# Attention gated by a token mixer on one core: one turn of four PSUM banks for scores and block products, block pairs spread over the steps in new orders, and a first chunk that is normalised in two halves

## The chip, the core and the metric

The kernel runs on one core of a Trainium2 chip. PE is the matrix engine, DVE the vector engine, ACT the scalar engine, POOL GpSimd, SP the engine whose queue issues most DMAs. The metric is the time of one execution on the device in microseconds, as the median of several runs. Durations inside the kernel come from one profiled execution.

## What is computed

S = 2048 tokens, D = 512 channels, 32 heads of 16, F = 1792. With xn = layernorm(x):

```python
s = attention(xn, wqkv) @ wo            # 32 heads, full softmax over 2048 keys, scale 16 ** -0.5
h = layernorm(xn)
u = gelu(einsum("sd,sf->df", h, w1) + b1)     # the MLP acts along the tokens
y = (einsum("df,fs->ds", u, w2) + b2).T
out = x + s * silu(y)
```

All is float32. Matrix products take each operand as an upper part (rounded for the matrix engine, F32R) and a lower part (the rest), and sum three products: upper by upper, upper by lower, lower by upper.

## The kernel before

**Stages.** (1) For each of four chunks of 512 tokens: normalise x on DVE (`Norm`), turn it with PE transposes (L268, `turned`), split it into `xt` (upper by ACT, lower by DVE), multiply by wq and wk (L303, eight groups of 12 products), split the results (`sg`) and store them; then the V products (`three`, L86 to L88). The weights' upper halves are copied by ACT, their lower halves subtracted by POOL (L79). (2) A lead of 11 steps in which row maxima of the first scores are found. (3) The steady part. (4) The drain: the remaining scores, values and products with wo. (5) The tail: the last pair of heads.

**A step of the steady part** covers two score tiles t (128 keys by 1024 queries, two heads a = 0, 1). It holds 8 score products (L777, called s: heads in the two row halves of the array, 50 rows each), each read by one exponential on ACT (L782); 8 products for row maxima of a later pair of heads (L394, called m), each read by one reduction on DVE (L398); twice the products with the values (L793, `values`), which use four column strips of the array; and up to six pairs of block matmuls (L944, called D, two row halves of 64). Two instructions in opposite row halves run side by side, so a step is written as two strings of letters, one for each half, which are read off in pairs; two indices in `ORDERS`, `ENDS` or `BEGINS` say where the values stand. `take` draws the block pairs from a generator, `count` says how many.

**Blocks.** `mixer` makes 14 blocks of the first MLP product (48 pairs each, `gelu`) and 16 of the second (42 pairs, `silu`). `rest` makes `PARTS` = 13 blocks of the attention's output product from the first three groups of heads (9 pairs, `part`, stored to `y_d`), and in the drain one product for each of 16 token blocks, 12 matmuls where no part was made, 3 where one was (`finish`, L753). A block adds up in one PSUM bank and is then emptied by ACT or DVE. At a block's end a step takes no further pairs.

**Banks.** PSUM has eight banks here: pools `ps_sc` (3, scores), `ps_mx` (3, maxima), `ps_av` (1, values), `ps_dn` (1, blocks). Stage 1 takes all eight in turn (`bank`).

**What sets the order.** The code is issued as written, each engine works off its queue in order, and semaphores order the engines. The step tables are written by hand. Lists `later` and `soon` hold work that `run_later` issues at the two places of a step.

Of the kernel before, what the change touches and what calls it, by code (L numbers as in the profile page):

```python
# [21 lines left out]
def tile_attention_token_mixer(ctx, tc, x, wqkv, wo, w1, b1, w2, b2, out):  # L22
# [131 lines left out]
    with (  # L154
        tc.tile_pool(name="pw", bufs=1) as pw,
        tc.tile_pool(name="px", bufs=5) as px,
        tc.tile_pool(name="pt", bufs=6) as pt,
# [23 lines left out]
        for part in range(3):  # L181
            for kd in range(ND):
                nm = ("raw", "wh", "wl")[(part * ND + kd) % 3]
# [4 lines left out]
        def w_upper(part):  # L188
            for kd in range(ND):
                nc.scalar.copy(wh[part][:, kd, :], raw_w[part, kd])  # L190

        def w_lower(part):
            for kd in range(ND):
                sub(nc.gpsimd, wl[part][:, kd, :], raw_w[part, kd], wh[part][:, kd, :])

        class Norm:


            def __init__(self, src, dst, then=None):
                self.src, self.dst, self.then = src, dst, then  # L200
# [7 lines left out]
            def rsqrt(self):  # L208
                ve = pst.tile([P, 4], F32, name="ve")
                r = self.r = pst.tile([P, 4], F32, name="r")  # L210
                t = pst.tile([P, 4], F32, name="t")
                nc.vector.tensor_scalar(ve, self.mv[:, :, 1], 1e-5, None, op0=OP.add)
                nc.scalar.sqrt(t, ve)
                nc.vector.reciprocal(r, t)
# [14 lines left out]
            def pieces(self):  # L229
                for b in range(4):  # L230
                    yield lambda b=b: self.stats(b)
                yield self.rsqrt
                for b in range(4):
                    yield lambda b=b: self.apply(b)

        def first(c):
# [4 lines left out]
            return Norm(lambda b: xr[4 * c + b], dst)  # L241
# [11 lines left out]
        def bank():  # L253

            i = turn_of[0] = (turn_of[0] + 1) % 8
            pl, nm = ((ps_sc, "sc"), (ps_mx, "mx"), (ps_dn, "dn"), (ps_av, "av"))[i % 2 if i < 6 else i - 4]
            return pl.tile([P, 512], F32, name=nm)

        for f in first(0).pieces():
            f()  # L260
        w_upper(0)
        xts_ = [[] for _ in range(NC)]

        def turned(c, db):
# [4 lines left out]
            t = pt.tile([P, 2, 512], F32R, name="xt")  # L269
            nc.scalar.copy(t[:, 0, :], ps)  # L270
            sub(nc.vector, t[:, 1, :], ps, t[:, 0, :])
            xts_[c].append(t)

        for c in range(NC):
            cs = slice(c * 512, (c + 1) * 512)
            for db in range(len(xts_[c]), ND):
                turned(c, db)
            if c == 0:

                nc.gpsimd.tensor_copy(pst.tile([P, 1], F32, name="hold"), xn[3][:, :1])  # L280
                w_upper(1)
                w_lower(0)
                w_lower(1)
# [5 lines left out]
            if c == 0:  # L289
                w_upper(2)  # L290
                w_lower(2)
# [35 lines left out]
            for f in todo[len(order) * per :]:  # L327
                f()
# [11 lines left out]
            pv = [bank()[:, :D] for _ in range(4)]  # L340
            if c + 1 < NC:
                for kd in range(ND):
                    for b in range(4):
                        v_product(b, kd)
                    if 0 < kd < ND - 1:
                        turned(c + 1, kd + 1)
            for b, ps in enumerate(pv):
# [5 lines left out]
                else:  # L353
                    v48 = pt.tile([P, 2, 512], F32R, name="xt").bitcast(F32).rearrange("p a b -> p (a b)")
                    v48 = v48[:, : NP * 48].rearrange("p (a b c) -> p a b c", b=3, c=DH)
                nc.gpsimd.memset(v48[:, :, 1, :], 1.0)
                nc.scalar.copy(v48[:, :, 0:3:2, :], ps.rearrange("p (a b c) -> p a b c", b=2, c=DH))
                nc.sync.dma_start(v_d[4 * c + b], v48.rearrange("p a b c -> p (a b c)"))
# [76 lines left out]
    def mixer():  # L435
        n = 0
        ub = []
        for i in range(NF + NB):
            nk = NB if i < NF else NF
            before = i < min(N_BEFORE, NF)  # L440
            if before and i % 2:
                ps = ps_av.tile([P, 512], F32, name="av")[:, :D]
            else:
                ps = ps_dn.tile([P, 512], F32, name="dn")[:, :D]
            for kb in range(nk):
# [5 lines left out]
                if i == NF and kb == NF - 1:  # L451
# [4 lines left out]
                    yield None  # L456
# [696 lines left out]
```

## Time and profile before

| | |
|---|---|
| median of 3 runs | 1667.26 us (1667.24 to 1667.9) |
| profiled execution | 1667.68 us, its span 1665.9 us |
| granted clock of PE, mean | 0.999 |
| PE busy | 1644.1 us, 11700 matmul records |
| DVE, ACT, POOL busy | 1426.0, 1194.2, 569.9 us |
| DMA | 155.30 MB, mean 93 GB/s |
| first chunk's PE work begins | 9.80 us |
| steady part | 216.40 to 1587.00 us |
| last value products begin | 1646.07 us |

The profile gives each group of instructions by line, engine, operation and names (out<-in), its busy time, the mean length of one in ns, and the idle time before it with what ended it. In the rows of stretches stand: the stretch and its length, then for each engine (PE, PE's weight loads PEld, DVE, ACT, POOL) busy time and number of instructions, the granted clock, the mean DMA share and GB/s. Rows in order of time give start, length, engine, line, names, shapes, count, and idle time with its releaser. A product with values shows as two matmul records, every other product as one.

### The profile page before, as it was taken

Reading aid. Unit: us, or ns where it says so; the run is one execution under the profiler, and the core shown is the slowest. Engines: PE = TensorE matmul, PEld = TensorE weight load, DVE = VectorE, ACT = ScalarE, POOL = GpSimd, SP = SyncE. Lnnn points to the kernel's source line nnn. Section 1 sums busy time; section 2 is a strip of 40 time slices with the busy share of each in tenths; the row PEclk is TensorE's granted clock in tenths of the full one; section 3 lists DMA queues with packets and bytes.
Section 4 is the critical chain, followed back from the end, with each engine's and each line's share of the span. In section 5 each row is a group of like instructions: output and inputs, shape, how many; then the busy total and the mean of one; then the engine's idle time right before and its main releaser. Section 6 shows DMA issues by size and latency. Waiting matters only on the chain.

```text
span 1665.9 us, 30703 instructions
## 1 busy us (share of the span) xinstructions
PE 1644.1 (99%) x11700; PEld 871.3 (52%) x11700; DVE 1426.0 (86%) x2482; ACT 1194.2 (72%) x2295; POOL 569.9 (34%) x671
## 2 busy tenths in 40 slices
PE   7999999999999999999999999999999999999997
PEld 6887645545545445554545454554545454444443
DVE  6555988888999899999999999999999999899945
ACT  3332277777777777777877777777777778888875
POOL 4223763433344332331322332222222322642420
PEclk9999999999999999999999999999999999999999
DMA  6468521415133141916151513224051515362346
GB/s 228 165 241 206 115 80 46 72 42 84 49 61 72 34 69 46 247 56 106 36 84 36 96 41 54 57 46 74 21 83 44 103 37 86 119 131 94 107 140 224
DMA packets 152175, 155.30 MB, mean 93 GB/s; under 512 B 51596, under 2 KB 109964, under 8 KB 148956
## 3 DMA queue, kind: packets, MB, share of 16 engines
q1 hardware_dynamic: 147612, 152.59, 38.1%
q8 instruction: 92, 1.51, 0.4%
q0 software_dynamic: 4416, 0.75, 0.3%
q14 instruction: 55, 0.45, 0.1%
HBM read 101.86 MB, written 50.32 MB: 91 GB/s over the span
## 4 chain that ended last, share of the span: by engine, by line
PE 96%; DVE 2%; DMA 1%; ACT 1%; issue 0%; POOL 0%; SPq 0%; DVEq 0%; POOLq 0%
PE av L793 30%; PE dn L944 23%; PE mx L394 17%; PE sc L777 13%; PE dn L903 3%; PE mx L303 2%; PE sc L303 2%; DVE mxp L398 1%; PE av L903 1%; PE dn L303 1%; PE av L303 1%; ACT prob L782 1%; PE mx L777 0%; PE sc L86 0%; PE sc L88 0%; PE sc L87 0%
## 5 line engine op out<-in xcount | busy, mean ns | idle before, releaser
L398 DVE TENSOR_REDUCE mxp<-mx 128x1 f32<-128x512 f32 x2004 | 1244.6, 684 | 134.9 <-PE mx L394 93.8
L782 ACT ACTIVATE prob<-sc 128x512 f32<-128x512 f32 x2004 | 1044.8, 605 | 296.2 <-PE sc L777 182.2
L777 PE MATMUL sc<-big 50*128 50x512 f32 x2004 | 755.6, 417 | 0.5
L394 PE MATMUL mx<-big 48*128 48x512 f32 x2004 | 738.6, 418 | 0.9
L793 PE MATMUL av<-prob,vp 128*32 128x512 f32 x4096 | 545.6, 605 | 0.0
L944 PE MATMUL dn<-hu,wh 64*128 64x512 f32 x1556 | 535.0, 404 | 0.0
L394 PEld LDWEIGHTS mx<-big 48*128 48x128 f32 x2004 | 358.6, 185 | 270.6 <-DVE mxp L398 248.7
L777 PEld LDWEIGHTS sc<-big 50*128 50x128 f32 x2004 | 358.6, 185 | 104.1 <-ACT prob L782 83.5
L944 PE MATMUL dn<-hu,wl 64*128 64x512 f32 x778 | 316.3, 407 | 0.0
L944 PEld LDWEIGHTS dn<-hu,wh 64*128 64x128 f32 x1556 | 284.4, 184 | 44.9 <-issue 23.8
L944 PEld LDWEIGHTS dn<-hu,wl 64*128 64x128 f32 x778 | 143.6, 185 | 108.1 <-issue 78.8
L793 PEld LDWEIGHTS av<-prob,vp 128*32 128x32 f32 x4096 | 80.9, 108 | 177.0 <-issue 166.1
L79 POOL TENSOR_TENSOR wl<-raw,wh 128x512 fp32r<-128x512 f32 x124 | 150.7, 1218 | 38.6 <-ACT wh L150 30.0
L148 POOL CAST wh<-raw 128x512 fp32r<-128x512 f32 (+1 forms) x107 | 62.1, 581 | 260.1 <-PE dn L944 177.7
L421 POOL CAST m<-f 16x128 fp32r<-16x128 f32 x32 | 9.0, 281 | 280.4 <-DVE f L410 280.4
L480 POOL TENSOR_TENSOR sq<-u 128x512 f32<-128x512 f32 x14 | 14.6, 1041 | 177.8 <-ACT u L479 177.8
L83 POOL DMA_DIRECT2D big<-m x128 | 67.7, 535 | 0.0
L944 PE MATMUL dn<-wh,hu 64*128 64x512 f32 x156 | 55.4, 408 | 0.0
L516 POOL TENSOR_SCALAR t<-t 128x512 f32<-128x512 f32 x16 | 23.8, 1490 | 79.9 <-ACT t L513 79.9
L79 POOL TENSOR_TENSOR hu<-hx,hu 128x512 fp32r<-128x512 f32 x16 | 20.3, 1291 | 53.5 <-ACT hu L246 53.5
L782 ACT ACTIVATE prob<-mx 128x512 f32<-128x512 f32 x44 | 28.1, 639 | 13.7 <-PE sc L777 13.6
L303 PE MATMUL mx<-xt,big 128*128 128x512 f32 x144 | 35.9, 399 | 0.0
(205 smaller groups left out, 1117.0 us busy)
## 6 DMA issues: line engine op xcount, KB each, us to landing
raw<-in_B_w_dram SPq DMA_DIRECT2D x104, 256.0 KB
big<-k_d SPq DMA_DIRECT2D x96, 128.0 KB
big<-q_d SPq DMA_DIRECT2D x96, 128.0 KB
q_d<-sg SPq DMA_DIRECT2D x16, 512.0 KB
k_d<-sg SPq DMA_DIRECT2D x16, 512.0 KB
num_d<-ev SPq DMA_DIRECT2D x30, 256.0 KB
u_d<-uo SPq DMA_DIRECT2D x14, 512.0 KB
hu<-u_d SPq DMA_DIRECT2D x14, 512.0 KB
```

What stands on the lines that cost most here:

```text
L79: eng.tensor_tensor(out=o, in0=a, in1=b.bitcast(F32), op=OP.subtract)
L83: queue.dma_start(dst.bitcast(F32), src.bitcast(F32))
L148: nc.gpsimd.tensor_copy(whs[n][:, :m, :], raws[n][:, :m, :])
L303: nc.tensor.matmul(ps, w[part][:, kd, m], xt[kd][:, z, :], start=w is wh and z == 0 and kd == 0, stop=w is wl and kd == ND - 1,)
L394: nc.tensor.matmul(ps, q[o : o + 48, r * P : (r + 1) * P], k[o : o + 48, c * 512 : (c + 1) * 512], start=True, stop=True,)
L398: nc.vector.tensor_reduce(mxp[u // 16][:, a, r % 8, c : c + 1], ps, axis=AX.X, op=OP.max)
L516: nc.gpsimd.tensor_scalar(t, t, 1.0, None, op0=OP.add)
L777: nc.tensor.matmul(ps, ks[p][o : o + 50, kb * P : (kb + 1) * P], qs[p][o : o + 50, at : at + 512], start=True, stop=True,)
L782: nc.scalar.activation(e, ps, AF.Exp, scale=scale)
L793: nc.tensor.matmul(av[32 * j : 32 * j + 32, :], vps[p][:, kb, 16 * a : 16 * a + 32], prob.pop((t, a, c)), start=kb == 0, stop=kb == NB - 1,)
L903: nc.tensor.matmul(ps, w(slice(0, P)), m(slice(0, P)), start=first, stop=last)
L944: made.append(lambda r=r, start=first and a == lead, stop=last and a != lead: nc.tensor.matmul(ps, w(r), m(r), start=start, stop=stop,))
```

## The change

1. **One turn of four banks.** `ps_dn` goes; `ps_sc` has four banks, each a pool of one, taken in turn. A block holds the bank that stands first in the turn (`hold`) and gives it back at the turn's end when the instruction that empties it is issued.
2. **Blocks over steps.** `count` spreads what is left of a block evenly over steps; only three blocks take six pairs in every step. The tables for a block's beginning and end go; `ORDERS` has new strings. The Tanh of `silu` is issued one `run_later` later. The last load of the second product's operand stands two rows earlier, two idle draws behind it go. `PARTS` is 14.
3. **The first chunk.** The V weights are loaded first. 36 transposes of the identity into an unused bank open PE's work (`busy`), some more stand between the first products. Token blocks 0 and 1 are normalised, turned (a block at a time, into all four rows of `xt`), split and multiplied by the V weights before blocks 2 and 3 have been turned. Eleven of twelve lower halves of the weights move from POOL to DVE. `xt` tiles are pairs (3 of double size for 6).

```diff
-    ps_sc = pool("ps_sc", 3, space=PSUM)
-    ps_mx = pool("ps_mx", 3, space=PSUM)
-    ps_av = pool("ps_av", 1, space=PSUM)
-    ps_dn = pool("ps_dn", 1, space=PSUM)
+    class Banks:
+        def __init__(self, name, n):
+            self.free = [pool(f"{name}{i}", 1, space=PSUM) for i in range(n)]
+        def tile(self, shape, dtype, name):
+            self.free.append(self.free.pop(0))
+            return self.free[-1].tile(shape, dtype, name=name, tag="ps")
+        def hold(self, name):
+            p = self.free.pop(0)
+            return p.tile([P, 512], F32, name=name, tag="ps"), lambda: self.free.append(p)
+    ps_sc = Banks("ps_sc", 4)
+    ps_mx = Banks("ps_mx", 3)
+    ps_av = Banks("ps_av", 1)
...
+        def block_turn(b):
+            ps = bank()
+            for db in range(ND):
+                nc.tensor.transpose(ps[:, db * P : (db + 1) * P], xn[b][:, db * P : (db + 1) * P], ident)
+            return ps
...
+        busy(36)
+        one, two = first(0, range(2)), first(0, range(2, 4))
+        for f in one.pieces():
+            f()
...
+        ps0 = block_turn(0)
+        ps1 = block_turn(1)
+        busy(8)
+        two.stats(2)
+        two.stats(3)
+        w_upper(2, [0])
+        block_upper(0, ps0)
+        two.root()
+        w_upper(2, [1])
+        block_lower(0, ps0)
+        w_upper(2, [2])
+        block_upper(1, ps1)
+        two.refine()
+        w_upper(2, [3])
+        for b in (2, 3):
+            two.apply(b)
+        block_lower(1, ps1)
+        w_lower(2, range(ND), nc.vector)
+        for kd in range(ND):
+            v_part(0, 0, wh, [kd])
+            busy((4, 4, 2, 0)[kd])
+        ps2 = block_turn(2)
+        v_part(1, 0, wh, range(ND))
+        ps3 = block_turn(3)
+        v_part(0, 1, wh, range(ND))
+        v_part(1, 1, wh, range(ND))
...
+        w_lower(0, range(1, ND), nc.vector)
+        w_upper(1)
+        w_lower(1, range(ND), nc.vector)
...
             if c == 0:
-                w_upper(2)
-                w_lower(2)
+                for b in range(2):
+                    v_out(b, pv[b], v48s[b], True)
                 nc.sync.dma_start(b1t, b1.rearrange("(b p) -> p b", p=P))
                 nc.sync.dma_start(b2t, b2.rearrange("(b p) -> p b", p=P))
                 nc.vector.tensor_scalar(b2h, b2t, 0.5, None, op0=OP.mult)
...
-                ps = ps_dn.tile([P, 512], F32, name="dn")[:, :D]
+                ps, back = ps_sc.hold("dn")
...
-                if i == NF and kb == NF - 1:
+                if i == NF and kb == NF - 3:
                     while NF - 1 not in stored:
                         yield None
                     ub.append(hu.tile([P, 2, D], F32R, name="hu"))
                     move(ub[NF - 1], u_d[NF - 1])
-                    yield None
-                    yield None
...
-        nc.scalar.activation(t, y, AF.Tanh)
+        later.append(lambda: nc.scalar.activation(t, y, AF.Tanh))
...
-    PARTS = NB // 2 + 5
+    PARTS = NB // 2 + 6
...
-    FULL = range(4, 8)
+    FULL = range(4, 7)
...
-        6: ("DDDDDDsmmsmsms", "msmssmmsDDDDDD", 4, 8),
+        6: ("DDDDDDsmsmsmsm", "smsmmsmsDDDDDD", 4, 8),
...
-        return 4 if late or left in (7, 8) else 5 if left == 9 else max(0, min(6, left))
+        if left == 9:
+            return 4
+        return min(6, -(-left // -(-3 * left // 16))) if left > 0 and i not in FULL else max(0, min(6, left))
```

What this moves in the engines' queues, at three places. First PE at the end of a 42-pair block, before: from the old block's last row to the first of the new one (dn is the block's bank, av the values, mx and sc the maxima and scores; rows of both halves in the order of issue).

```order
L944 MATMUL dn<-hu,wl 128x512
L793 MATMUL av<-prob,vp 32x512 x4
L394 MATMUL mx<-big 128x512
L777 MATMUL sc<-big 128x512 x2
L394 MATMUL mx<-big 128x512
L777 MATMUL sc<-big 128x512
L394 MATMUL mx<-big 128x512
L793 MATMUL av<-prob,vp 32x512 x4
L394 MATMUL mx<-big 128x512
L777 MATMUL sc<-big 128x512
L944 MATMUL dn<-hu,wh 128x512
```

The same place after, with buffer numbers, since the two blocks' rows would read alike (L1050 is the block matmul, L892 a score, L510 a maximum):

```order
L1050 MATMUL dn_14940<-hu_10155,wh_15028 128x512
L510 MATMUL mx_15595<-big_1398,big_1397 128x512
L1050 MATMUL dn_14940<-hu_10155,wl_15029 128x512
L1050 MATMUL dn_15602<-hu_8915,wh_15263 128x512
L892 MATMUL sc_15610<-big_1397,big_1398 128x512
L1050 MATMUL dn_15602<-hu_8915,wh_15263 128x512
L510 MATMUL mx_15615<-big_1398,big_1397 128x512
L1050 MATMUL dn_15602<-hu_8915,wl_15264 128x512
L892 MATMUL sc_15619<-big_1397,big_1398 128x512
```

The new block's first matmul (dn_15602) now follows the old one's last (dn_14940) at once, where two groups of products with values and eight others stood between them.

Second, PE at the start, before:

```order
L268 MATMUL mx<-ident,xn 128x128 x4
L268 MATMUL sc<-ident,xn 128x128 x4
L268 MATMUL mx<-ident,xn 128x128 x4
L268 MATMUL sc<-ident,xn 128x128 x4
L303 MATMUL mx<-xt,big 128x512 x12
L303 MATMUL dn<-xt,big 128x512 x12
```

And after (L331 are transposes of the identity, L304 those of a token block, L344 V products, L412 the products with wq and wk):

```order
L331 MATMUL mx<-ident 128x128 x36
L304 MATMUL sc<-ident,xn 128x128 x4
L304 MATMUL mx<-ident,xn 128x128 x4
L331 MATMUL mx<-ident 128x128 x8
L344 MATMUL sc<-wvh,xt 128x512
L331 MATMUL mx<-ident 128x128 x4
L344 MATMUL sc<-wvh,xt 128x512
```

Twenty-four V products and the turning of blocks 2 and 3 now stand ahead of the first group of twelve.

Third, DVE around the scaling of b2 (`b2h`), which waits for a small DMA. Before:

```order
L222 TENSOR_SCALAR xn<-xr,mv,r 128x512 x4
L79 TENSOR_TENSOR xt<-mx,xt 128x512
L79 TENSOR_TENSOR xt<-sc,xt 128x512
L79 TENSOR_TENSOR xt<-mx,xt 128x512
L79 TENSOR_TENSOR xt<-sc,xt 128x512
L294 TENSOR_SCALAR b2h<-b2t 128x16
L79 TENSOR_TENSOR sg<-mx,sg 128x512
```

After:

```order
L94 TENSOR_TENSOR big<-wl,big 128x512
L94 TENSOR_TENSOR big<-raw,big 128x512
L94 TENSOR_TENSOR big<-wh,big 128x512
L94 TENSOR_TENSOR big<-wl,big 128x512
L403 TENSOR_SCALAR b2h<-b2t 128x16
L94 TENSOR_TENSOR sg<-sc,sg 128x512
```

Lower halves of the weights (big, wvl) now stand in DVE's queue ahead of `b2h`, and the load of b2 stands behind two stores of v in SP's queue.

More of the change, by code (lines that the diff above doesn't have):

```diff
@@ L229, in pieces, with first @@
             def pieces(self):
-                for b in range(4):
+                for b in self.some:
                     yield lambda b=b: self.stats(b)
                 yield self.rsqrt
-                for b in range(4):
+                for b in self.some:
                     yield lambda b=b: self.apply(b)
-        def first(c):
+        def first(c, some=range(4)):
             def dst(b):
@@ new lines, in v_out, with busy @@
+        def v_out(n, ps, v48, ones_in=False):
+            if not ones_in:
+                nc.gpsimd.memset(v48[:, :, 1, :], 1.0)
+            nc.scalar.copy(v48[:, :, 0:3:2, :], ps.rearrange("p (a b c) -> p a b c", b=2, c=DH))
+            nc.sync.dma_start(v_d[n], v48.rearrange("p a b c -> p (a b c)"))
+        v48s = [pst.tile([P, NP, 3, DH], F32, name="v48", bufs=2) for _ in range(2)]
+        for v48 in v48s:
+            nc.gpsimd.memset(v48[:, :, 1, :], 1.0)
+        idle = bank()
+        def busy(n):
+            for _ in range(n):
+                nc.tensor.transpose(idle[:, :P], ident, ident)
@@ new lines, in tile_attention_token_mixer, with v_part @@
+        busy(36)
+        one, two = first(0, range(2)), first(0, range(2, 4))
+        for f in one.pieces():
+            f()
+        pair = [pt.tile([P, 2, 2, 512], F32R, name="xt") for _ in range(2)]
+        xts_[0] = [pair[db // 2][:, db % 2] for db in range(ND)]
+        done_db[0] = ND
+        pv = [bank()[:, :D] for _ in range(2)]
+        def v_part(b, z, w, kds):
+            for kd in kds:
+                nc.tensor.matmul(
+                    pv[b], xts_[0][kd][:, z, b * P : (b + 1) * P], w[2][:, kd, :],
+                    start=w is wh and z == 0 and kd == 0, stop=w is wl and kd == ND - 1,
+                )
@@ L1000, in tile_attention_token_mixer @@
             steady[0] = True
-            late = ended[0]
-            one, two, then = halves(lead, count(late))
+            one, two, then = halves(lead, count())
             made = [dict(D=part, m=heads[a][0], s=heads[a][1]) for part, a in ((one, lead), (two, 1 - lead))]
-            first, second, *places = order(len(one), t, late, bool(then))
+            first, second, *places = order(len(one))
             if one:
@@ L1018, in tile_attention_token_mixer @@
                         of[kind].pop(0)()
-                if "D" in kinds and not two:
-                    for f in then:
-                        f()
-                    then = []
             for f in then:
```

152 lines of the change are left out of this document (84 added, 68 removed).

## The prediction, made before the changed kernel was run

> **What bounds the kernel now.** I read the page first, then the busy time stage by stage, then the order of time on PE, ACT and DVE at a block's end, at the start and near the end. The page, with columns as in its legend:
>
> ```profile
> span 1665.9 us, 30703 instructions
> ...
> PE 1644.1 (99%) x11700; PEld 871.3 (52%) x11700; DVE 1426.0 (86%) x2482; ACT 1194.2 (72%) x2295; POOL 569.9 (34%) x671
> ...
> PE 96%; DVE 2%; DMA 1%; ACT 1%; issue 0%; POOL 0%; SPq 0%; DVEq 0%; POOLq 0%
> ...
> L398 DVE TENSOR_REDUCE mxp<-mx 128x1 f32<-128x512 f32 x2004 | 1244.6, 684 | 134.9 <-PE mx L394 93.8
> L782 ACT ACTIVATE prob<-sc 128x512 f32<-128x512 f32 x2004 | 1044.8, 605 | 296.2 <-PE sc L777 182.2
> ```
>
> PE carries the chain. But its busy time is modelled and overlapping, so 99% does not say that no time is lost: what counts is the pitch of its matmuls. The steady part, from the first attention products at 216.40 to 1587.00, cut at block ends; first all engines, then the block matmuls (L944) alone:
>
> ```profile
> 216.40:269.52 53.12, 53.00 (x399) 26.41 (x398) 47.05 (x80) 40.64 (x80) 19.64 (x23) 1.00 0.17 51
> 269.52:407.43 137.91, 137.91 (x1058) 70.00 (x1056) 122.15 (x208) 104.54 (x203) 53.55 (x63) 1.00 0.31 61
> 407.43:709.99 302.56, 302.39 (x2301) 151.24 (x2299) 272.90 (x467) 231.94 (x448) 109.80 (x132) 1.00 0.38 84
> 709.99:770.89 60.90, 60.58 (x439) 28.26 (x439) 54.88 (x93) 47.52 (x93) 18.96 (x23) 1.00 0.27 60
> 770.89:1436.23 665.34, 665.08 (x5068) 332.43 (x5067) 607.44 (x1034) 521.61 (x1004) 200.33 (x252) 1.00 0.34 66
> 1436.23:1587.00 150.77, 149.96 (x1105) 70.28 (x1104) 138.25 (x236) 125.96 (x244) 65.98 (x65) 1.00 0.40 107
> ```
>
> ```profile
> 216.40:269.52 53.12, 28.98 (x104) 17.91 (x104) 1.00 0.17 51
> 269.52:407.43 137.91, 79.52 (x289) 49.73 (x288) 1.00 0.31 61
> 407.43:709.99 302.56, 157.82 (x578) 100.78 (x577) 1.00 0.38 84
> 709.99:770.89 60.90, 25.09 (x88) 15.14 (x88) 1.00 0.27 60
> 770.89:1436.23 665.34, 343.12 (x1256) 219.48 (x1256) 1.00 0.34 66
> 1436.23:1587.00 150.77, 65.57 (x238) 42.82 (x238) 1.00 0.40 107
> ```
>
> Each step holds 16 halves of scores and maxima and 16 products with values, so (all minus L944)/32 is the number of steps: 9, 24, 54, 11, 119, 27, in all 244. Half of the L944 count is block pairs, some 1276. Now one 42-pair block's length with its end, on PE, DVE and ACT (start, length):
>
> ```profile
> 1268.53 1.06 PE L793 MATMUL av<-prob,vp 128*32 128x512 f32 x8
> ...
> 1296.95 1.07 PE L793 MATMUL av<-prob,vp 128*32 128x512 f32 x8
> ...
> 1302.21 1.06 PE L793 MATMUL av<-prob,vp 128*32 128x512 f32 x8
> ...
> 1304.76 0.39 PE L944 MATMUL dn<-hu,wl 64*128 64x512 f32 x1
> ...
> 1308.33 0.40 PE L944 MATMUL dn<-hu,wh 64*128 64x512 f32 x1
> ...
> 1313.23 1.06 PE L793 MATMUL av<-prob,vp 128*32 128x512 f32 x8
> ```
>
> ```profile
> 1298.52 4.94 DVE L398 TENSOR_REDUCE mxp<-mx 128x1 f32<-128x512 f32 x8 [0.51 <-PE mx L394]
> ```
>
> ```profile
> 1305.70 0.71 ACT L512 ACTIVATE ev<-dn,b2h 128x512 f32<-128x512 f32 x1
> 1306.44 0.63 ACT L513 ACTIVATE t<-ev 128x512 f32<-128x512 f32 x1
> ```
>
> From 1268.53 to 1296.95 lie five six-pair steps: 5.68 us each. A warm 512-wide matmul takes 0.227 (rows of the start, below). My yardstick for a step without loss is 5.68, less 0.227 for each pair short of six. A 42-pair block, eight steps long (1268.53 to 1313.23), took 44.70; by the yardstick 45.44 - 6 x 0.227 = 44.08. So 0.62 is lost, all at the block's end: the old block's last matmul starts at 1304.76, the new one's first only at 1308.33, because both use the one dn bank, which ACT empties at 1305.70; the Tanh behind it keeps ACT from the exponentials.
>
> The same sum by stage (steps x 5.68 - missing pairs x 0.227, against the length): lost 1.8, 1.6, 4.7, 3.6, 8.7 and 6.9, together 27.3 us. That is all that banks and orders can win here. The fourth stage, the change from first to second weights, is where steps hold 1 or 2 pairs.
>
> **The change, part by part.**
>
> Banks. The next block takes the score bank that has been free longest, the old one goes last in the turn. It no longer waits for ACT's emptying. What is late next: scores. While a block is open they have three banks, as before; at a block's end their turn begins with the bank of the last step's seventh of eight scores. By the new order its score stands some 0.9 us ahead of its next use; from the matmul's start to the end of the exponential I take about 0.45 (a matmul's 0.39, 1304.76, and a hand-over) + 0.6 (L782's mean), so 0.1 to 0.2 us is lost. The third score, on the emptied bank, stands behind the next product with values, over 2 us later, and ACT's 0.71 fits. I take 0.2 for each of 40 block ends (1 + 3 + 7 + 16 + 13): 8.0. Bounds: 0, and 0.62 as now.
>
> Tanh one turn later: the same ACT work, under the products with values; nothing of its own.
>
> Spread and orders. The number of steps is the same. The 42 pairs go 6, 6, 5, 5, 5, 5, 5, 5 instead of 6 x 6, 4, 2. A five-pair step by the yardstick is 5.45, above DVE's eight reductions in a row (4.94, the row at 1298.52). DVE is busy 607.44 of 665.34 and stays below PE. In the new orders for five and for six pairs the maxima stand five in a row at two-slot distance, then three behind the product with values, as in the old six-pair order whose steps are the yardstick; so I take no loss for them. Bounds: 0 and 0.1 a step, what a 5.45 step would lose if reductions and the 0.6 of transposes beside them came in a bad place. One block (the eighth) goes from eight steps to nine, the change of weights from about 1.5 pairs a step to full steps, so the steps come out even; its 3.6 goes too.
>
> Parts (last stage): 14 blocks of 9 pairs instead of 13, alternating 4 and 5. Beside the block ends I leave 2.8 here, for ACT's copies of quotients, which stay where they are. Steady part: 27.3 - 8.0 - 2.8 = 16.5 won. The 4 pairs more that now fit into it cost 4 x 0.227 = 0.9. The added part block's copy (ACT, about 0.6), two POOL operations, a load pair and a store on SP's queue lie under PE; the DMA share there is 0.40.
>
> The start. Rows of POOL, DVE and PE:
>
> ```profile
> 1.01 0.29 POOL masks.py:199 TENSOR_SCALAR_AFFINE_SELECT ident<-ident 128x128 f32<-128x128 f32 x1
> ```
>
> ```profile
> 4.94 0.18 DVE L206 BATCH_NORM_AGGREGATE mv<-st 128x2 f32<-128x6 f32 x1
> ...
> 7.66 0.17 DVE L212 TENSOR_SCALAR ve<-mv 128x4 f32<-128x4 f32 x1
> ...
> 9.12 1.91 DVE L222 TENSOR_SCALAR xn<-xr,mv,r 128x512 f32<-128x512 f32 x4
> ...
> 22.22 0.29 DVE L294 TENSOR_SCALAR b2h<-b2t 128x16 f32<-128x16 f32 x1 [6.75 <-DMA b2t<-in_B_b_dram]
> ...
> 31.41 0.54 DVE L222 TENSOR_SCALAR xn<-xr,mv,r 128x512 f32<-128x512 f32 x1
> ```
>
> ```profile
> 9.80 1.75 PE L268 MATMUL mx<-ident,xn 128*128 128x128 f32 x4 [9.80 <-DVE xn L222]
> ...
> 12.21 1.06 PE L268 MATMUL mx<-ident,xn 128*128 128x128 f32 x4
> 13.06 1.06 PE L268 MATMUL sc<-ident,xn 128*128 128x128 f32 x4
> ...
> 17.81 2.89 PE L303 MATMUL dn<-xt,big 128*128 128x512 f32 x12
> ...
> 36.87 0.60 PE L268 MATMUL mx<-ident,xn 128*128 128x128 f32 x4
> ```
>
> Twelve products take 2.89 at 17.81, the last of them some 0.39, so 0.227 each. But the first transposes go at 0.213 (four in 0.85), twice the later length (0.60 against 1.06 for four): 9.80 to about 16.4 runs at half pace. With two blocks normalised first, the variance follows the second aggregate: 5.15; the first block is 1.46 behind (as 9.12 after 7.66), 6.6; PE 0.68 behind, 7.3. The 36 idle transposes start when the identity is there (1.01 + 0.29), about 1.4 us. If they need the same 6.6 us, 31 go at 0.213 and five at half that: they end at 8.5, and block 0 starts then. From there ACT decides: two copies for each block and three weight copies at about 0.6 put the last upper V product of block 0 near 12.5. DVE does the second half's normalisation, the lower halves and four V weights (0.6 each, taken from POOL) to about 15.7. The 24 V products of blocks 0 and 1 end near 18.1. Before, 12 products were done at 17.81. So 12 x 0.227 - 0.3 = 2.4 won.
>
> By the Trainium skill ("TensorE: Matmul & The Clock Gate", Part 1, "What you observe") the clock opens some 4 us into sustained matmul activity. The trace shows about 6.6 us in a start with gaps; by the page's 4 the idle transposes would end near 7.2, the start would win 3.1 and the total would be 0.7 lower (estimate from that page).
>
> What is queued behind a wait: b2h stands in DVE's queue ahead of every sg. Its load is now issued behind the two stores of v, about 5.4 us later, so DVE stands until some 27.6 instead of 22.2. The cover is that the next chunk's transposes also come later (36.87 becomes about 39.8) and that DVE had that chunk normalised at 31.95, 4.9 ahead of PE. I cost it at nothing; if the cover fails, 1 to 2 us. Bounds of the start: +1 and -4.
>
> The end. Rows of PE:
>
> ```profile
> 1623.82 1.06 PE L793 MATMUL av<-prob,vp 128*32 128x512 f32 x8
> ...
> 1628.91 1.07 PE L793 MATMUL av<-prob,vp 128*32 128x512 f32 x8
> ...
> 1642.87 0.50 PE L903 MATMUL dn<-wh,hu 128*128 128x512 f32 x1 [0.39 <-DVE gt L753]
> ```
>
> A block of 12 matmuls becomes one of 3: 9 x 0.227 = 2.0, and it is on the path, since a step of 5.09 exceeds its eight exponentials (8 x 0.5). The wait of 0.39 for DVE goes with the single bank. Won: 2.4 (bounds 0.4 and 2.5).
>
> Sum on the profiled execution: 1665.9 - 16.5 + 0.9 - 2.4 - 2.4 = 1645.5; it ran 1667.68, 1.8 around the span, and the median is 0.4 lower: 1646.9, about 1647.
>
> **The rivals.**
> 1. Block ends cost nothing: 8.0 + 2.8 more, and the start 1 more: 1635. For it: ACT is busy 78% in the fifth stage. Against: the score turn above is short by 0.1 to 0.2.
> 2. The new orders stumble: 0.07 to 0.1 us in each of some 190 steps with new places, 13 to 19 us: the steady gain is gone, the start and end remain, 1660 to 1665. For it: the five-pair step leaves DVE only 0.5 us. Against: the same burst of maxima runs in the old six-pair step.
> 3. Slower: the emptied block bank is in the scores' turn, so a score can now wait for ACT's emptying, and PE, in order, stands with maxima and values behind it. If emptying, Tanh and a copy of a quotient come in a row (0.71 + 0.63 + 0.6) ahead of it, 1.5 us at each of 40 ends is 60, less 31 won: about 1697. It decides from 31/40 = 0.8 us an end. Against: the Tanh is moved away and that score stands over 2 us later.
> 4. The start does not do what it says: half pace stays through the V products (24 x 0.2 = 4.8, half of it under waits) or DVE is late for chunk 1: start +1, total 1650.
>
> **How the numbers follow.** My forecast, 1640 to 1652, has 0.55; rival 1 has 0.14, rival 2 0.14, rival 3 0.06, rival 4 0.11 (inside the range). The range 1638 to 1660 leaves out rival 3, half of rivals 1 and 2. Under 0.2% (3.3 us) cannot be told from no change here. Slower: 0.07 (rival 3 and 0.01 of rival 2); the same: 0.05 (the worst of rival 2); faster: 0.88.
>
> **What would show it.** By order of time: the new block's first matmul within 0.5 us of the old one's last; steps of five pairs at 5.45; no step of 1 or 2 pairs near 750; the first V product before 10 and Q/K products from about 18; sum of steady part about 1355. Wrong if scores wait for ACT's emptying at block ends, or five-pair steps take 5.6.

## The result, and the profile after

The changed kernel takes 1651.62 us (median of 4 runs, 1648.49 to 1652.96) against 1667.58 us for the kernel before on the same chip: a ratio of 0.9902, 95% interval 0.9884 to 0.9919. The forecast was 1647 with a range of 1638 to 1660. The profiled execution is the quickest of the four: 1648.49 us, with a span of 1646.7 us, 19.2 below the 1665.9 of before. The page's head and the shares of its chain:

```profile
span 1646.7 us, 30923 instructions
...
PE 1632.0 (99%) x11758; PEld 879.8 (53%) x11758; DVE 1424.4 (86%) x2503; ACT 1186.7 (72%) x2301; POOL 557.0 (34%) x662
...
PE 93%; DMA 3%; DVE 1%; POOL 1%; ACT 1%; SPq 1%; issue 0%; DVEq 0%; POOLq 0%; ACTq 0%
```

PE does about the same work as before in 12 us less of modelled busy time, and 3% of the chain is now a DMA where it was 1%. That points to the place that went wrong, since from 1601 to 1626 us the chain runs through loads and stores; the share is no measure of it, since the second profile of this kernel (again, below) has 1% with the same wait. The steady part by stretches (columns as in the table of before):

```profile
212.36:265.40 53.04, 53.04 (x411) 27.44 (x414) 47.37 (x81) 39.36 (x78) 20.32 (x24) 1.00 0.16 51
265.40:410.00 144.60, 144.60 (x1116) 75.19 (x1108) 129.29 (x221) 110.54 (x216) 53.38 (x63) 1.00 0.34 64
410.00:760.00 350.00, 350.00 (x2695) 177.10 (x2696) 319.29 (x548) 271.96 (x530) 132.38 (x159) 1.00 0.36 81
760.00:1400.00 640.00, 640.00 (x4925) 323.52 (x4925) 586.62 (x1006) 503.49 (x975) 191.76 (x244) 1.00 0.33 65
1400.00:1567.72 167.72, 167.01 (x1239) 80.36 (x1235) 153.36 (x261) 138.14 (x270) 70.20 (x69) 1.00 0.42 112
```

It runs from 212.36 to 1567.72, 1355.36 us, where before took 1370.60. PE is busy to the last hundredth in the first four stretches; before it was not in any but the second. A block's end, on PE and on ACT (start, length):

```profile
1106.43 0.39 PE L1050 MATMUL dn<-hu,wl 64*128 64x512 f32 x1
1106.67 0.39 PE L1050 MATMUL dn<-hu,wh 64*128 64x512 f32 x1
1106.80 0.50 PE L892 MATMUL sc<-big 50*128 50x512 f32 x1
...
1107.94 1.07 PE L908 MATMUL av<-prob,vp 128*32 128x512 f32 x8
```

```profile
1106.14 1.09 ACT L897 ACTIVATE prob<-sc 128x512 f32<-128x512 f32 x2 [0.55 <-PE dn L1050]
1107.12 0.69 ACT L627 ACTIVATE ev<-dn,b2h 128x512 f32<-128x512 f32 x1
```

The old block's last matmul starts at 1106.43 and the new one's first 0.24 later, where 3.57 lay between them before. The score at 1106.80 has 0.50, not 0.39: it comes late, about when ACT ends the first of the two exponentials from 1106.14. That costs this block's end 0.24: from the values at 1104.38 to those at 1107.94 stand nine pairs of instructions, which take 3.56, where a stretch of ten takes 3.55 and each pair some 0.235. ACT empties the old bank while PE works on the new one.

The start, on PE, and one row of DVE:

```profile
1.36 5.70 PE L331 MATMUL mx<-ident 128*128 128x128 f32 x36 [1.36 <-POOL ident masks.py:199]
...
8.98 0.48 PE L344 MATMUL sc<-wvh,xt 128*128 128x512 f32 x1
...
17.65 2.66 PE L412 MATMUL sc<-xt,big 128*128 128x512 f32 x11
...
46.66 1.52 PE L412 MATMUL sc<-xt,big 128*128 128x512 f32 x6
```

```profile
26.70 0.17 DVE L403 TENSOR_SCALAR b2h<-b2t 128x16 f32<-128x16 f32 x1 [5.80 <-DMA b2t<-in_B_b_dram]
```

The second chunk's products with wq and wk begin at 46.66; in the kernel before, its row is

```profile
49.64 1.52 PE L303 MATMUL mx<-xt,big 128*128 128x512 f32 x6
```

The end, on SP's queue, DVE and PE:

```profile
1619.20 0.36 SPq L871 DMA_DIRECT2D out_dram<-u  x1
...
1622.78 0.32 SPq L862 DMA_DIRECT2D u<-y_d  x1
...
1623.46 0.32 SPq L864 DMA_DIRECT2D sq<-g_d  x1
```

```profile
1626.54 0.69 DVE L868 TENSOR_TENSOR sq<-dn,sq 128x512 f32<-128x512 f32 x1 [3.02 <-DMA sq<-g_d]
```

```profile
1624.52 0.50 PE L892 MATMUL mx<-big 50*128 50x512 f32 x1
...
1627.29 0.50 PE L892 MATMUL sc<-big 50*128 50x512 f32 x1 [2.27 <-DVE sq L868]
1627.72 2.78 PE L908 MATMUL av<-prob,vp 128*32 128x512 f32 x24
```

Read from below: the last score stands 2.27 us, until DVE has emptied a block's bank; DVE stands 3.02 until the gate `sq` has come; its load was issued only at 1623.46, because in `load_out` it stands behind the load of `u` from `y_d`, and that one behind the store that still reads the buffer of `u` (issued at 1619.20). The same delay of DVE was in the kernel before, 2.79 us long:

```profile
1646.33 0.69 DVE L753 TENSOR_TENSOR sq<-dn,sq 128x512 f32<-128x512 f32 x1 [2.79 <-DMA sq<-g_d]
```

There the late bank was the block's own, and only the next block would have waited.

### The profile page after: what moved, and what is told of

It reads as the page before. It is cut to its first block, busy times and chain, and to the rows that moved or that the text cites. A ratio compares the mean times of both kernels' runs of the same rounds, so it can differ in the third digit from the quotient of the medians.

```text
span 1646.7 us, 30923 instructions
## 1 busy us (share of the span) xinstructions
PE 1632.0 (99%) x11758; PEld 879.8 (53%) x11758; DVE 1424.4 (86%) x2503; ACT 1186.7 (72%) x2301; POOL 557.0 (34%) x662
## 4 chain that ended last, share of the span: by engine, by line
PE 93%; DMA 3%; DVE 1%; POOL 1%; ACT 1%; SPq 1%; issue 0%; DVEq 0%; POOLq 0%; ACTq 0%
PE av L908 30%; PE dn L1050 24%; PE sc L892 16%; PE mx L510 13%; PE sc L412 3%; PE mx L412 2%; PE dn L1021 1%; PE av L412 1%; DMA raw<-in_B_w_dram 1%; PE sc L101 0%; PE sc L103 0%; PE sc L102 0%; DMA out_dram<-u 0%; DMA big<-k_d 0%; ACT prob L897 0%; PE mx L103 0%
## 5 line engine op out<-in xcount | busy, mean ns | idle before, releaser
L510 PE MATMUL mx<-big 48*128 48x512 f32 x2004 | 761.0, 416 | 0.0
L892 PE MATMUL sc<-big 50*128 50x512 f32 x2004 | 739.7, 411 | 2.8 <-DVE sq L868 2.3
L1050 PE MATMUL dn<-hu,wh 64*128 64x512 f32 x1556 | 530.4, 408 | 0.0
L892 PEld LDWEIGHTS sc<-big 50*128 50x128 f32 x2004 | 358.8, 186 | 242.6 <-ACT prob L897 222.8
L510 PEld LDWEIGHTS mx<-big 48*128 48x128 f32 x2004 | 357.7, 186 | 162.4 <-DVE mxp L514 145.4
L1050 PEld LDWEIGHTS dn<-hu,wh 64*128 64x128 f32 x1556 | 277.1, 184 | 90.7 <-issue 64.9
L1050 PE MATMUL dn<-hu,wl 64*128 64x512 f32 x778 | 308.3, 396 | 0.0
L1050 PEld LDWEIGHTS dn<-hu,wl 64*128 64x128 f32 x778 | 143.5, 184 | 13.2
L1050 PE MATMUL dn<-wh,hu 64*128 64x512 f32 x162 | 53.1, 394 | 0.0
L412 PE MATMUL sc<-xt,big 128*128 128x512 f32 x192 | 46.1, 389 | 0.0
L412 PEld LDWEIGHTS sc<-xt,big 128*128 128x128 f32 x192 | 36.0, 188 | 7.5
```

The source lines that it names most:

```text
L412: nc.tensor.matmul(ps, w[part][:, kd, m], xt[kd][:, z, :], start=w is wh and z == 0 and kd == 0, stop=w is wl and kd == ND - 1,)
L510: nc.tensor.matmul(ps, q[o : o + 48, r * P : (r + 1) * P], k[o : o + 48, c * 512 : (c + 1) * 512], start=True, stop=True,)
L892: nc.tensor.matmul(ps, ks[p][o : o + 50, kb * P : (kb + 1) * P], qs[p][o : o + 50, at : at + 512], start=True, stop=True,)
L1050: made.append(lambda r=r, start=first and a == lead, stop=last and a != lead: nc.tensor.matmul(ps, w(r), m(r), start=start, stop=stop,))
```

## The experiments

Two questions: where the 4.7 us between forecast and median lie, and which part of the change wins what. The table has all runs. Steady length and end are of the profiled execution; the cut between them is in every kernel at the same work, ahead of the last 192 records of products with the values.

| kernel | median us (range) | ratio to before, 95% | steady us | end us |
|---|---|---|---|---|
| before | 1667.58 | 1 | 1370.60 | 78.9 |
| changed | 1651.62 (1648.49 to 1652.96) | 0.9902 [0.9884, 0.9919] | 1355.36 | 79.0 |
| again | 1650.90 (1648.69 to 1652.13) | 0.9900 [0.9885, 0.9914] | 1355.43 | 78.9 |
| gate_first | 1647.02 (1646.24 to 1647.47) | 0.9877 [0.9863, 0.9892] | 1355.64 | 76.7 |
| drain_busy | 1649.28 (1648.75 to 1649.53) | 0.9892 [0.9877, 0.9906] | 1354.90 | 79.1 |
| old_start | 1652.59 (1651.14 to 1655.32) | 0.9915 [0.9899, 0.9932] | 1355.78 | 79.9 |
| start_only | 1664.84 (1663.94 to 1666.27) | 0.9985 [0.9975, 0.9994] | 1370.47 | 79.0 |
| no_idle | 1649.66 (1648.05 to 1650.72) | 0.9893 [0.9879, 0.9908] | 1356.41 | 76.7 |
| own_bank | 1692.41 (1691.40 to 1692.72) | 1.0149 [1.0133, 1.0164] | 1399.35 | 78.9 |
| uneven | 1666.86 (1665.93 to 1667.51) | 0.9996 [0.9987, 1.0006] | 1375.48 | 76.7 |
| uneven_paired | 1672.62 (1672.38 to 1673.19) | 1.0032 [1.0020, 1.0045] | 1381.76 | 76.7 |
| parts13 | 1648.06 (1647.29 to 1648.61) | 0.9884 [0.9867, 0.9900] | 1354.64 | 78.2 |
| tanh_now | 1647.17 (1646.34 to 1648.03) | 0.9878 [0.9864, 0.9893] | 1354.92 | 76.8 |

**again**: the changed kernel as it is.

> The changed kernel once more, unchanged. Its four runs lay between 1648.5 and 1653.0 us, those of the kernel before within 0.7 us. Both theories: median 1650 to 1652 again, runs scattered over some 4 us. Theory D (the drain): the scatter is PE's wait for a score bank that a product with wo still holds, because DVE waits for a late load of the gate from DRAM (2.3 us in the profiled execution); a profile of a slower run shows this wait longer, or PE's clock closed after it. Theory S (the start): the scatter is PE's clock in the first 20 us; a profile of a slower run has its Q/K products begin later than 17.65.

1650.90, with the same wait (2.32 us) in its profile. Over both sets the two profiled executions, at a mean granted clock of 0.999, are the two quickest; the six others took 1650.8 to 1653.0 at 0.997 or 0.998. The clock belongs to the story. Neither profile is of a slower execution, so this run alone doesn't decide between the two theories.

**gate_first**: in `load_out` the gate's load is issued ahead of that of y.

```diff
         y, g = (("xt", "gt"), ("u", "sq"))[n % 2]
+        gts[b] = el.tile([P, D], F32, name=g)
+        nc.sync.dma_start(gts[b], g_d[b])
         if n >= NB // 2:
             ys[b] = el.tile([P, D], F32, name=y)
             nc.sync.dma_start(ys[b], y_d[b])
-        gts[b] = el.tile([P, D], F32, name=g)
-        nc.sync.dma_start(gts[b], g_d[b])
```

> The changed kernel with two loads of the drain exchanged: for each token block the load of the gate is issued ahead of the load of the kept sum, which waits for an earlier store. Theory D: the wait of 2.3 us of a score for DVE near the end is gone or under 0.3, the median falls by 2 to 5 us to 1646 to 1649 and the scatter shrinks to about 1 us. Theory S: the best run falls by about 2 us, but the scatter of some 4 us stays.

1647.02, 3.9 below again on the same chip and 4.6 below the first set, with every run at 0.999. Its DVE and PE at the same place:

```profile
1623.94 0.69 DVE L868 TENSOR_TENSOR sq<-dn,sq 128x512 f32<-128x512 f32 x1 [0.91 <-PE dn L1021]
```

```profile
1625.72 0.50 PE L892 MATMUL mx<-big 50*128 50x512 f32 x1
1625.72 0.50 PE L892 MATMUL sc<-big 50*128 50x512 f32 x1
```

DVE waits for the block's products alone, and the last two scores go side by side. The wait and its cause are shown: two lines in another order take it away, and the end gets 2.2 to 2.3 us shorter. That is somewhat more than half. This kernel has the lowest median of all that were run; tanh_now, with the same order of loads, can't be told from it.

**drain_busy**: the rest. The wait stays, but PE is kept busy in it.

```diff
                 made[1][i]()
+                if s == total - 2 and i == n - 1:
+                    spare = ps_mx.tile([P, 512], F32, name="mx")
+                    for _ in range(20):
+                        nc.tensor.transpose(spare[:, :P], ident, ident)
                 made[0][i]()
```

> The changed kernel with 20 transposes of the identity, into a bank of the maxima, ahead of the last score, which waits 2.27 us at 1627.29. They take 20 x 0.107 = 2.1 us, under the wait, so the wait stays. Theory K (the wait makes a stretch of 3.41 us in which PE works little, and when that stretch falls badly the clock closes for 3.41 us; this puts the median of the changed kernel 3 us above its quickest run): granted clock 0.999 in every run, median 1648.0 to 1649.0 with a spread under 1.5 us. Rival: the scatter comes from elsewhere: 1650 to 1652, clocks 0.997 to 0.998 in most runs.

1649.28, a spread of 0.8 us, all runs at 0.999. The last score still comes 2.83 after its partner (1625.43 to 1628.26), the end is as long as in the changed kernel (79.1), and yet the median is 1.6 to 2.3 lower than the two of the changed kernel, and the scatter gone. (The median lies 0.3 above the range that I gave.) So filling PE's wait removes the rest, and with it the lower clocks: the reading is that the clock closes in most executions of the changed kernel because PE does too little around this wait. No profile of the changed kernel shows it closed there; that of old_start (below), which has the wait too, does. Its rows of two stretches next to each other:

```profile
1626.05:1629.47 3.42, 1.87 (x14) 0.52 (x10) 1.30 (x2) 2.96 (x7) 0.00 (x0) 1.00 0.97 372
1629.47:1632.88 3.41, 3.41 (x20) 0.85 (x16) 0.09 (x1) 0.60 (x1) 0.00 (x0) 0.50 0.62 225
```

In the first, where the last score comes after a wait of 1.55,

```profile
1628.88 0.49 PE L791 MATMUL sc<-big 50*128 50x512 f32 x1 [1.55 <-DVE sq L767]
```

PE is busy 1.87 of 3.42 us; in the second the granted clock is 0.50, from 1629.47 for 3.41 us. In all profiles of the case the times between changes in the trace's clock record are whole multiples of 3.413 us, so the stretches form a grid. On the changed kernel's own grid its wait falls across two of them:

```profile
1622.51:1625.92 3.41, 2.51 (x16) 0.91 (x15) 0.98 (x2) 2.80 (x6) 0.00 (x0) 1.00 0.54 183
1625.92:1629.33 3.41, 2.04 (x17) 0.73 (x21) 1.38 (x2) 1.33 (x3) 0.00 (x0) 1.00 0.68 263
```

2.51 and 2.04 of 3.41 were enough, and the clock stayed open in this execution. Where the grid lies changes from run to run. The Trainium skill ("TensorE: Matmul & The Clock Gate", Part 1, "What's actually happening") says that the window is free-running and 3413 ns long, which the traces confirm, and that the clock falls back after at least one idle window; here the clock fell back after one in which PE was 55% busy by its modelled rows.

**old_start**: the changed kernel with the first chunk of before. **start_only**: the reverse, the kernel before with the new first chunk. Both swap these lines, what follows them up to the first group of products, and what the first chunk needs with them (tiles, the order of the weights, its V products):

```diff
-        busy(36)
-        one, two = first(0, range(2)), first(0, range(2, 4))
-        for f in one.pieces():
-            f()
...
```

> The changed kernel with the first chunk as it was before: banks, spread, orders and 14 parts stay. If the pieces of the change add up, the start's 4.0 us (steady part begins at 212.4 instead of 216.4) come back: best run about 1652.5, median 1653 to 1656, steady part at 15.2 us less than before. Theory D: the scatter of some 4 us stays. Theory S: it shrinks to under 1 us.

> The kernel before with the new first chunk alone. If the pieces add up: 1663 to 1664 us, steady part begins 3 to 4 us earlier and is as long as before, 1370.6. Theory D: scatter under 1 us, as before. Theory S: scatter of some 4 us.

The new start is worth 2.7 us on the kernel before (1664.84 against 1667.50, ratio 0.9985), near the 2.4 forecast. On the changed kernel it is worth 1.7 (1652.59 against 1650.90 of again), but both scatter by the clock; in the profiles the steady part starts at 214.29 with the old start and at 212.36 with the new one, 1.9 apart. Both medians miss the ranges set for these runs by 0.4 to 0.8, since those took the whole 4.0 between the two profiles for the start's.

These two runs also say where the scatter comes from. With the old start and the wait at the end it is 4.2 us; with the new start and the old end it is 2.3 over ten runs, as in the kernel before beside it (2.4 over 13). It goes with the end, not with the start.

**no_idle**: gate_first without the 54 idle transposes.

```diff
-        busy(36)
...
-        busy(8)
...
-            busy((4, 4, 2, 0)[kd])
```

> The kernel with the gate load first, without the 54 transposes of the identity at the start (36 ahead of the first block, 18 between products). Then PE's first work is the first block's transposes near 7.1 to 7.7, at half pace. Theory G (activity with gaps opens the clock too, 6.6 us after its beginning as in the kernel before, 9.80 to 16.4): open near 14, most of the half pace lies under waits for ACT, products with wq and wk from 17.6 to 18.6, total 1647 to 1648. Theory S (only activity without gaps opens it, some 4 us): the 16 dense products from 13.8 on run at half pace, 16 x 0.2 = 3.2 more, products with wq and wk from about 20.8, total 1650 to 1651.

1649.66, 2.6 above gate_first and between the two theories. PE's rows:

```profile
7.25 1.08 PE L304 MATMUL sc<-ident,xn 128*128 128x128 f32 x4 [7.25 <-DVE xn L246]
...
11.76 0.79 PE L338 MATMUL sc<-wvh,xt 128*128 128x512 f32 x1 [0.27 <-ACT wvh L205]
...
13.05 2.06 PE L338 MATMUL mx<-wvh,xt 128*128 128x512 f32 x4
...
15.62 1.27 PE L338 MATMUL sc<-wvh,xt 128*128 128x512 f32 x4
...
19.45 2.88 PE L404 MATMUL sc<-xt,big 128*128 128x512 f32 x12
```

Four V products take 2.06 at 13.05 and 1.27 at 15.62: half pace lasts until about 15.8, 8.6 us after PE's first work, and products with wq and wk begin at 19.45 instead of 17.59. PE's last wait ahead of that ends at 11.76, 4 us before the clock opens. That is against G, whose 6.6 us would end at 13.9, and fits S only if its last gap is put two us earlier than I had it. The grid tells more than either. In the trace's clock record the first change, to the full clock, stands at 15.81, and the two stretches of the grid ahead of it read:

```profile
8.98:12.40 3.42, 2.59 (x6) 1.17 (x6) 3.20 (x13) 2.33 (x7) 0.00 (x0) 1.00 0.76 291
12.40:15.81 3.41, 3.41 (x14) 2.92 (x13) 3.29 (x7) 0.65 (x2) 0.19 (x1) 1.00 0.37 127
```

In all thirteen profiles the clock opens in this way, at the end of the first stretch in which PE is busy nearly throughout: 3.15 to 3.41 us in the stretch that opened it, at most 3.12 in those ahead of it. So it depends on where the grid lies when PE's dense work begins. The limit can't be read closer, since PE's lengths are modelled.

**own_bank**: the changed kernel with three score banks and a bank of their own for blocks, as before the change.

```diff
-    ps_sc = Banks("ps_sc", 4)
+    ps_sc = Banks("ps_sc", 3)
+    ps_dn = Banks("ps_dn", 1)
...
-                ps, back = ps_sc.hold("dn")
+                ps, back = ps_dn.tile([P, 512], F32, name="dn"), lambda: None
```

> The changed kernel with a bank of the blocks' own, as before (three score banks in turn and one dn bank); spread, orders, start and 14 parts stay. Theory T (the turn of four banks is what lets the new orders run): a new block's first matmul now waits for ACT's emptying of the old block, some 1.2 us at each of 40 block ends: 1690 to 1702 us. Rival (the orders alone bring the gain, the emptying is hidden): 1650 to 1655.

1692.41, 1.5% slower than the kernel before. PE's waits (in total, times, longest):

```profile
PE dn L1051 <- ACT ev L628: 17.0, 15, 1.1
PE dn L1051 <- ACT t L829: 12.3, 13, 0.9
PE dn L1051 <- ACT u L595: 11.3, 10, 1.2
```

38 waits, 40.6 us, 1.07 each. The steady part is 44.0 longer than in the changed kernel's profile, so the waits are nine tenths of it. (The medians differ by 40.8, but most executions of the changed kernel ran at a lower clock than its profile.) With a bank of the blocks' own, even blocks and the new orders are not worth less, they lose: the new block's first matmul stands right behind the old one's last, and with PE in order everything behind it waits for ACT.

**uneven**: gate_first with blocks of 6, ..., 6, 4, 2 pairs, the bank turn kept, and as many steps.

```diff
-        return min(6, -(-left // -(-3 * left // 16))) if left > 0 and i not in FULL else max(0, min(6, left))
+        if left == 6 and sizes[i] % 6 == 0 and i not in FULL and i < len(sizes) - PARTS:
+            return 4
+        return max(0, min(6, left))
```

> gate_first (1647.0) with a block's pairs as unevenly spread as before: 6 pairs in each step and 4 and 2 in the last two; banks and orders of the change. 23 blocks. If DVE limits a step of few pairs (eight reductions in a row took 4.94, a two-pair step is 4.77 by the yardstick, and the transposes come on top), 0.2 to 0.5 is lost a block: 1652 to 1659. Rival (the spread does not matter, banks and orders do): 1646 to 1648.

A miss: 1666.86, no better than the kernel before, 20 us above gate_first; I had expected 5 to 12. By the list of its waits PE waits for nothing in the steady part; its matmuls are just further apart, in the step with the short draw, in each of 23 blocks (0.86 each). One reason lay in my edit: a step of two pairs used the string for four, so that two slots hold one half alone, 0.45 us by the price of a slot. That leaves as much again, and in the short step of 1073.35 two scores wait for ACT's exponentials (0.24 at 1076.05 and 0.19 at 1076.54, in PE's weight loads).

**uneven_paired** mends that with strings of ten and eleven slots from the kernel before.

```diff
     ORDERS = {
...
+        2: ("mmsmDDsssm", "ssmsmsmmDD", 3, 10),
+        3: ("DDDsssmmsmm", "ssmmmmssDDD", 4, 7),
```

> As uneven (gate load first, blocks of 6, ..., 6, 4, 2 pairs instead of even ones), but steps of two and of three pairs use the strings of the kernel before, ten and eleven slots long. In uneven a step of two pairs used the string for four, so that two of its twelve slots hold one half alone: 2 x 0.227 = 0.45 us in each of 23 blocks, 10 us. Theory O (only these slots and their neighbours were lost; spreading as such is worth little): 1648 to 1657. Theory E (a short step cannot be faster than its eight reductions of 4.94 us and what stands beside them, so the even spread is what wins): 1662 to 1668.

1672.62: worse still, beyond both ranges. The cause of theory E is there, but it is not the only one. DVE, then PE at a short step, then two of PE's weight loads with what they waited for:

```profile
1072.07 5.54 DVE L514 TENSOR_REDUCE mxp<-mx 128x1 f32<-128x512 f32 x9 [0.26 <-PE sc L892]
```

```profile
1074.68 0.49 PE L510 MATMUL mx<-big 48*128 48x512 f32 x1
...
1075.27 0.50 PE L510 MATMUL mx<-big 48*128 48x512 f32 x1
...
1075.87 0.50 PE L510 MATMUL mx<-big 48*128 48x512 f32 x1
```

```profile
1075.27 0.18 PEld L510 LDWEIGHTS mx<-big 48*128 48x128 f32 x1 [0.41 <-DVE mxp L514]
...
1078.52 0.18 PEld L892 LDWEIGHTS sc<-big 50*128 50x128 f32 x1 [0.45 <-ACT prob L897]
```

Nine reductions run without a pause, 0.62 each, and the maxima follow one another at 0.59 to 0.60 on PE: here DVE sets the pace. From the values at 1072.40 to those at 1076.30 this costs some 0.8 us (3.91 for eight pairs of instructions, at 0.235 for each pair more or less than the ten that take 3.55). The next stretch, to 1079.67, loses some 0.5 more, and there two scores wait for ACT's exponentials. Less the 0.24 that a block's end costs in the changed kernel, that is the 1.1 us a block by which the steady part is longer. So a short step presses on DVE and on ACT, since its eight reductions and eight exponentials come closer together; theory E had only the first. In gate_first the eight reductions of a five-pair step fit:

```profile
1105.08 4.95 DVE L514 TENSOR_REDUCE mxp<-mx 128x1 f32<-128x512 f32 x8 [0.49 <-PE mx L510]
```

**parts13** and **tanh_now** undo one line each in gate_first.

```diff
-    PARTS = NB // 2 + 6
+    PARTS = NB // 2 + 5
```

```diff
-        later.append(lambda: nc.scalar.activation(t, y, AF.Tanh))
+        nc.scalar.activation(t, y, AF.Tanh)
```

> gate_first (1647.0) with 13 part blocks as before instead of 14. If the drain is bound by PE, 9 matmuls come back there (+2.0) and 4 pairs leave the steady part (-0.9): about 1648.1. Rival (the end waits for exponentials or loads, not for PE): 1646 to 1647.

> gate_first (1647.0) with the Tanh of silu issued at once, as before. If the emptied bank's score stands far enough behind, the Tanh costs nothing: 1646 to 1648. Rival (the exponentials behind it come late and scores wait for their banks): 0.2 to 0.5 at each of 16 block ends, 1650 to 1655.

The fourteenth part is worth 1.0 us by the medians (1648.06 against 1647.02: forecast 2.0 in the drain less 0.9 in the steady part), which is within the intervals of the two. In the profiles it costs 1.0 in the steady part and wins 1.4 in the end. The later Tanh is worth nothing that shows (1647.17).

## Why the prediction was right, and where it was not

**Steady part: right in size.** 16.5 won less 0.9 was forecast, 15.2 came (1370.60 to 1355.36). By the yardstick 11.1 us are lost now (244 steps, 1280.5 pairs), 10.8 was the forecast; a block's end costs 0.24, not 0.2; five-pair steps take 5.41 to 5.45; the new block's first matmul comes 0.24 after the old one's last. The losses by stage that the prediction lists don't all follow from its rows: with its whole numbers of steps they come out as 2.5, 1.5, 3.8, 3.4, 8.9 and 7.2. Their sum, 27.2, is the same within 0.1, and only the sum was used.

**Its reason was too narrow.** The step "0.62 is lost, all at the block's end ... because both use the one dn bank" holds the loss in the right place, but not the cause. In the kernel before PE had no wait for ACT on a block's bank; it was written around that wait, with short steps and late beginnings. PE's weight loads at the block's end of the prediction show what was lost instead:

```profile
1304.42 0.18 PEld L777 LDWEIGHTS sc<-big 50*128 50x128 f32 x1 [0.45 <-ACT prob L782]
...
1312.56 0.18 PEld L394 LDWEIGHTS mx<-big 48*128 48x128 f32 x1 [0.19 <-DVE mxp L398]
```

A score waits for an exponential, a maximum for a reduction. By the pace of the full stretches some 0.36 of the 0.62 lie where scores wait for ACT (1304.42, and 1309.20 with 0.21), and some 0.21 where this maximum waits for DVE. That is one block's end; over all of them the split wasn't measured.

The four runs make a square, all with the new start: own bank and uneven blocks 1664.8 (start_only), the turn with uneven blocks 1666.9 (1672.6 with paired strings), own bank with even blocks 1692.4, both new 1647.0 (the second and the last with the gate's load first). Neither half wins alone. Even blocks need a next block that begins at once, and only the turn allows that; the turn wins nothing while short steps are bound by DVE and ACT. The square isn't clean: start_only has 13 parts and the old tables for a block's beginning and end, which the uneven kernels lack, so better strings for the turn with short steps aren't excluded. The forecast took the sum from the yardstick, which is blind to the cause; that its size came out right is in this sense luck.

**Start: right.** 2.4 was forecast; the second chunk's products begin 2.98 earlier (49.64 to 46.66), and start_only won 2.7. Against old_start, where they begin at 48.79, it is 2.1: with the same first chunk as before the clock opened there at 14.97, in the kernel before at 16.34. The wait of `b2h` (until 26.70) cost nothing, as costed. By the Trainium skill ("TensorE: Matmul & The Clock Gate", Part 1, "What you observe") and its 4 us until the clock opens, the estimate was 3.1. The 36 transposes took 5.70 here, which with 0.213 and 0.107 each puts the opening about 3.4 us after the first one, close to that (the clock record has 3.2); in gate_first it was later:

```profile
1.36 6.76 PE L331 MATMUL mx<-ident 128*128 128x128 f32 x36 [1.36 <-POOL ident masks.py:199]
```

That is some 5.5 us, more than the page has, with products with wq and wk at 17.59 all the same: a later opening, still under the 36 transposes, did not delay them. Between the chunks and the steady part another 1.0 was won that was not forecast (the lead took 61.27 instead of 62.31); a wait of 0.2 to 1.2 us for POOL's lower halves of weights varies there from run to run, and with the new start and its idle transposes the steady part begins between 212.35 and 213.66, so I don't put it down to the change.

**End: the step that failed** is "the wait of 0.39 for DVE goes with the single bank". It grew to 2.27 and moved to a score, and the end got 0.1 longer instead of 2.4 shorter. The mechanism was in the text as rival 3, a score that waits for the emptying of a bank in the turn, but priced only at ACT's block ends in the steady part. DVE's late gate (2.79) was in the profile of the kernel before, and I had not asked who shares the bank it holds once the bank joins the turn. With the gate's load first the end shortens by 2.1, near the forecast.

The end's other term, 9 x 0.227 = 2.0, was too large. Only four of the added part's nine products fit into the steady part, as forecast; the other five run as whole products at the drain's start, and no term has them:

```profile
1568.71 0.50 PE L1021 MATMUL dn<-wl,hu 128*128 128x512 f32 x1
```

They cost some 0.6, part of them under waits: from the cut to the first product of twelve it is 9.81 us instead of 9.23. 2.0 less 0.6 is the 1.4 by which the ends of gate_first and parts13 differ.

**The median**: from the span, 1645.5 forecast, 1646.7 measured, the miss is 1.2. It is so small by luck: the end missed 2.5, and 1.6 that start and lead won beyond the forecast hide most of it. The other 3.1 lie between the profiled execution and the median, which drain_busy puts down to the clock around the same wait, and 0.4 I had taken off for the median. I had no term for that; the kernel before, with 0.39 of wait, has its stretch there busy for 3.04 of 3.42 us, and its clock open. The median lies at the very edge of the forecast of 1640 to 1652.

Rival 1 (ends cost nothing) and rival 2 (orders stumble) are out: 0.24 an end, five-pair steps at the yardstick. Rival 4's half pace did not come; in no_idle, without the idle transposes, it lasts until 15.8, well into the V products.

## What to carry to other kernels

Before a buffer that was private joins a shared turn, list every place where it is emptied late, with its price: a delay that nobody saw becomes a wait of whoever shares the turn, and at the end of a queue it may hang on the order of two loads. When two parts of a change are prices of the same constraint (here a private bank and short steps around it), test them apart before calling one of them the gain. When a kernel scatters more than its neighbours, look at the granted clock of each run and for a stretch in which the matrix engine does about half its work, and fill that stretch as a test.

## What the hardware showed that I had not expected

The clock closed after a stretch that was 55% busy (1.87 of 3.42 us), with one wait of 1.55 us in it, and then for one stretch of 3.41 us; stretches with 2.04 to 2.51 of 3.41 left it open. So a wait well below one stretch is enough, if it falls badly; the changed kernel, which has such a wait, differs by 2 to 4 us from run to run, and by 0.8 with the wait filled. The share of modelled busy time alone doesn't decide, though. In tanh_now's profile a stretch of the grid with no more than that left the clock open:

```profile
1636.29:1639.71 3.42, 1.86 (x9) 1.17 (x7) 3.42 (x7) 0.00 (x0) 2.16 (x2) 1.00 0.52 197
1639.71:1643.12 3.41, 0.00 (x0) 0.00 (x0) 2.17 (x4) 0.00 (x0) 0.00 (x0) 1.00 0.92 344
```

Its products stand as 128*128 in the rows, those of old_start's stretch as 50*128 and 128*32; whether that is the reason no run shows. How long the clock stays closed in the slower executions of the changed kernel itself was not seen, since both of its profiles caught it open.

At a span's start the granted clock (third number from the end) reads 1.00 while PE runs at half pace, in no_idle with four products in 2.06:

```profile
11.50:15.80 4.30, 4.04 (x14) 3.37 (x15) 4.19 (x10) 0.85 (x3) 0.19 (x1) 1.00 0.30 104
```

The record begins with its first change; ahead of that, pace has to be read from the rows.
